# A long convolution with a small expert: two 1,024-blocks, folded transforms, mirrored tables and a list-scheduled order

## The chip, the cores and the metric

The kernel runs on one core of one Trainium2 chip. The metric is the device time of one execution in microseconds (us); lower is better. Each kernel that matters was run several times, in rounds in which the kernel before ran on the same chip.

Engines: PE is TensorE (PEld its weight loads), DVE is VectorE, ACT is ScalarE, SP issues the DMAs (SPq is its sequencer). "L374" is line 374 of the kernel. The first lines of helper functions stand for all their callers: L374 is every DVE product or sum of two tensors in the changed kernel, L385 every ACT operation.

## The reference, cut to what matters

```python
def _A_ref(u, A_re, A_im, B_re, B_im, C_re, C_im, log_dt, Dskip):   # u: 1 x 2048 x 512
    dt = jnp.exp(log_dt)[:, None]
    ...
    P = jnp.exp(logdA[:, :, None] * l[None, None, :])               # 512 channels x 128 states x 2048 lags
    K = jnp.einsum("dn,dnl,dn->dl", Cc, P, dB).real                 # a filter of 2048 lags for each channel
    ...                                                             # y = u convolved with K, by FFT
    y = y.transpose(0, 2, 1) + u * Dskip[None, None, :]
def _B_ref(x, w_r, w_gate, w_up, w_down):
    idx = jnp.argsort(-(x @ w_r), axis=-1)[:, :2]                   # the 2 rows that go to the expert
    ...                                                             # silu(x w_gate) * (x w_up), then w_down
g = _sigmoid((x * gate_w).sum(-1, keepdims=True))
return g * a + (1 - g) * b
```

Both kernels build K from two tables. A lag is written as t1 + t2 with 32 values of t1 and 21 of t2; exp(lag x) is then a product of a t1 entry and a t2 entry, and the sum over the 128 states is a matrix product over partitions. Each entry needs an exp (magnitude), a sine and a cosine (angle) and two products. Then u and K are transformed, multiplied and transformed back.

## The kernel before

Its helpers keep one record of the last write and of the readers for each buffer; an operation waits for all that the record says:

```python
class Sched:
    def _deps(self, eng, reads, writes):
        ...
        for b in reads:
            add(b.last_w)
        for b in writes:
            add(b.last_w)          # one record for the whole buffer
            for r in b.readers:
                add(r)
    ...
    def op(self, eng, fn, reads=(), writes=()):
        waits = self._deps(eng, reads, writes)
        ...                        # program order is the order of each engine
```

The tables, four lags at a time, with a ring of two angle groups; and the table matmuls, one channel for each weight load, four of them beside each other in 32-column strips:

```python
elif stage == 'exp':
    for i, t in enumerate(lags):
        ...
        ACTV(TP(0, 128, (slot0 + i) * 8, (512, HC // 8), (1, 8)), AL(0, 128, c0, (1, HC)), ACTF.Exp, [bAL], [bTP], scale=float(t))
...
def kgen_mm(hh):
    ...
    h.matmul(P32(b, 32 * c4, 32, cq * 24, (1, 24)), TP(0, 128, (ch // 8) * 512 + (ch % 8), (8, 32)),
             TQ(0, 128, ch, (HC, 24)), start=True, stop=False, tile_position=(0, 32 * c4))
```

All 32 exps of the first half write `bTP` (those of the second another buffer, `bEB`), so each waits for the one before, although they write different columns.

Of the kernel before, what the change touches and what calls it, by code (L numbers as in the profile page):

```python
# [27 lines left out]
class Buf:  # L28

    def __init__(self, name, parents=()):  # L30
        self.name = name
        self.last_w = None
        self.readers = []
        self.parents = list(parents)

    def prior(self):
        out = []
        for p in self.parents:
            if p.last_w is not None:
                out.append(p.last_w)  # L40
            out.extend(p.readers)
            out.extend(p.prior())
        return out


class Sched:
    def __init__(self, nc, block_sems):
        self.nc = nc
        self.ops = {e: [] for e in ENGS}
        self.sem = dict(block_sems)  # L50
        self.cnt = {e: 0 for e in ENGS}
        self.known = {e: {} for e in ENGS}
        self.dma_sems = []
        self.dma_free = []
        self.final_waits = []

    def _deps(self, eng, reads, writes):
        deps = {}
        def add(ev):
            if ev is None:  # L60
                return
            s, v = ev
            k = id(s)
            if self.known[eng].get(k, 0) >= v:
                return
            if k not in deps or deps[k][1] < v:
                deps[k] = (s, v)
        for b in reads:
            add(b.last_w)
        for b in writes:  # L70
            add(b.last_w)
            for r in b.readers:
                add(r)
            for r in b.prior():
                add(r)
        out = list(deps.values())
        for s, v in out:
            self.known[eng][id(s)] = v
        return out

    def _commit(self, ev, reads, writes):
        for b in reads:
            b.readers.append(ev)
        for b in writes:
            b.last_w = ev
            b.readers = []

    def op(self, eng, fn, reads=(), writes=()):
        waits = self._deps(eng, reads, writes)
        self.cnt[eng] += 1  # L90
        ev = (self.sem[eng], self.cnt[eng])
        self.ops[eng].append((fn, waits, (self.sem[eng], 1)))
        self._commit(ev, reads, writes)
        return ev

    def dma(self, fn, sem, n=1, reads=(), writes=(), eng=SP, final=False):
        waits = self._deps(eng, reads, writes)
        ev = (sem, 16 * n)
        self.ops[eng].append((fn, waits, (sem, 16)))
        self._commit(ev, reads, writes)  # L100
        if final:
            self.final_waits.append(ev)
        return ev

    def emit(self, eng, h):
        for fn, waits, inc in self.ops[eng]:
            for s, v in waits:
                h.wait_ge(s, v)
            r = fn(h)
            if isinstance(r, (list, tuple)):  # L110
                for i in r:
                    i.then_inc(inc[0], inc[1])
            else:
                r.then_inc(inc[0], inc[1])
        if eng == SP:
            for s, v in self.final_waits:
                h.wait_ge(s, v)


def sb(t, p0, npart, col, *dims):  # L120
    w = t.shape[1]
    ap = [[w, npart]] + [[s, c] for (s, c) in dims]
    return bass.AP(t, p0 * w + col, ap)


# [3 lines left out]


LQ_T1 = [8 * k for k in range(32)]
LQ_T2 = list(range(8)) + [256, 258, 260, 262, 264, 516, 520, 772, 776, 1032, 1288, 1544, 1800]
NSLOT = 24
BLK, NBLK = 512, 4
KUSE = [(0, 0), (0, 1), (0, 2), (0, 3), (1, 3), (1, 4), (2, 4), (3, 4), (3, 5)]
# [9 lines left out]
def theta():  # L145
    f = np.arange(BLK)
    return 2.0 * np.pi * (f + 0.5) / (2 * BLK)


def fwd_mats():  # L150
    th = theta(); t = np.arange(BLK)
    c = np.cos(np.outer(t, th)); s = -np.sin(np.outer(t, th))
    sg = np.where(np.arange(BLK) % 2 == 0, 1.0, -1.0)[None, :]
    return np.concatenate([c, s], 1), np.concatenate([-sg * s, sg * c], 1)


def inv_mat():
    th = theta(); t = np.arange(BLK)
    c = (2.0 / (2 * BLK)) * np.cos(np.outer(th, t)); s = -(2.0 / (2 * BLK)) * np.sin(np.outer(th, t))
    return np.concatenate([c, s], 0)  # L160


def kspec_mats(L=2048):
    lq = bf16_lag(np.arange(L))
    rep = {}
    for j, t2 in enumerate(LQ_T2):
        for k, t1 in enumerate(LQ_T1):
            q = t1 + t2
            if q not in rep:
                rep[q] = (j, k)  # L170
    th = theta()
    out = np.zeros((len(KUSE), 128, 2 * BLK))
    cover = np.zeros(L, dtype=bool)
    for u, (i, jg) in enumerate(KUSE):
        for g in range(4):
            j = 4 * jg + g
            if j >= len(LQ_T2):
                continue
            for k in range(32):
                q = LQ_T1[k] + LQ_T2[j]  # L180
                if rep.get(q) != (j, k):
                    continue
                ls = np.nonzero(lq == q)[0]
                ls = ls[(ls >= BLK * i) & (ls < BLK * (i + 1))]
                if len(ls) == 0:
                    continue
                cover[ls] = True
                t = ls - BLK * i
                out[u, 32 * g + k, :BLK] = np.cos(np.outer(t, th)).sum(0)
                out[u, 32 * g + k, BLK:] = -np.sin(np.outer(t, th)).sum(0)  # L190
    assert cover.all(), "some lags are not covered by KUSE"
    return out



L, D, NS = 2048, 512, 128
NTB, NCH, NF, HC = 16, 4, 1792, 256


class View:  # L200

    def __init__(self, arena, byte_off, nbytes, dt):
        a = arena[:, byte_off // 2:(byte_off + nbytes) // 2]
        self.base = a if dt == BF else a.bitcast(dt)
        self.row = self.base.ap[0][0]

    def __call__(self, p0, npart, col, *dims):
        return bass.AP(self.base.tensor, self.base.offset + p0 * self.row + col, [[self.row, npart]] + [[s, c] for (s, c) in dims])


def bass_gated_mix__ssm_conv_s4__moe_arch_mod__prompt_kernel(nc, A_u, A_A_re, A_A_im, A_B_re, A_B_im, A_C_re, A_C_im, A_log_dt, A_Dskip,
           B_x, B_w_r, B_w_gate, B_w_up, B_w_down, gate_w, out, dbg=None):
    dbg = dbg or {}
    ident_c = nc.inline_tensor(bf16_bits(np.eye(128, dtype=np.float32)), "c_ident").ap().bitcast(BF)
    cf = np.zeros((128, 160), np.float32)
# [19 lines left out]
    with ExitStack() as es:  # L235
# [115 lines left out]
        def kt(i):  # L351
            return KPT(0, 128, i * D, (1, D))
# [572 lines left out]
```

## Time and profile before

| | before |
|---|---|
| time | 375.66 us (375.5 to 375.82) |
| span of the profiled run | 373.4 us |
| DVE busy | 270.7 us, 72%, 495 instructions |
| ACT busy | 239.4 us, 64%, 385 |
| PE busy | 188.9 us, 51%, 3,674 |

The prediction below shows the engine shares, the slices and the durations. Two more lines of the kernel before, from its list of the costliest groups: after the names stand the count, then busy us and mean ns, then the idle time just ahead of the group and who ended it.

```profile
L670 PE MATMUL ps<-RT 128*32 128x24 bf16 x512 | 22.7, 286 | 52.1 <-DVE RT L306 52.1
...
L403 ACT ACTIVATE RT<-RS 128x256 int32<-128x256 f32 x64 | 26.4, 416 | 1.9
```

The first is half of the table matmuls: they wait 52 us for DVE's tables and are small. The second is part of the angle work: 64 scalings on ACT, beside 148 more on DVE.

### The profile page before, as it was taken

To read this page: it belongs to the slowest core of one execution; us is meant where nothing else is said; L and a number is where in the kernel's file an instruction comes from. 1 tells how busy PE (TensorE), PEld (TensorE's weight loads), DVE (VectorE), ACT (ScalarE), POOL (GpSimd) and SP (SyncE) were. 2 spreads that over 40 slices of the span, in tenths; PEclk is the share of its full clock that TensorE was granted. 3 is DMA by queue.
4 is the path that set the end of the run, shared out by engine and by line. 5 is a ranking of instruction groups with operands and counts; after the bars stand their busy time and mean duration, and the time that the engine had idled before them with its cause. 6 is when DMAs were issued, how large, how long until landed. Compare 5 with 4: busy or idle time off the path is not lost.

```text
span 373.4 us, 8503 instructions
## 1 busy us (share of the span) xinstructions
PE 188.9 (51%) x3674; PEld 170.3 (46%) x3674; DVE 270.7 (72%) x495; ACT 239.4 (64%) x385; POOL 1.7 (0%) x6
## 2 busy tenths in 40 slices
PE   2600301432300076704343803889899999998810
PEld 2500300330100076704343703789889889886810
DVE  0795658562599992878105999999999299899555
ACT  2899453399596999566999981553753484481461
POOL 0000010000000000000000000000000000000000
PEclk9855555555655556855856865689989969969785
DMA  6999000005000000000000000000000000200222
GB/s 154 275 443 438 26 3 0 0 11 187 0 1 0 0 4 5 2 1 2 1 2 0 2 0 2 4 4 4 2 2 2 3 2 2 58 3 2 58 67 45
DMA packets 18261, 16.91 MB, mean 45 GB/s; under 512 B 12848, under 2 KB 17072, under 8 KB 18096
## 3 DMA queue, kind: packets, MB, share of 16 engines
q1 hardware_dynamic: 18224, 16.37, 13.3%
q8 instruction: 29, 0.48, 0.5%
q14 instruction: 8, 0.07, 0.1%
HBM read 14.27 MB, written 2.10 MB: 44 GB/s over the span
## 4 chain that ended last, share of the span: by engine, by line
ACT 36%; DVE 32%; PE 26%; issue 4%; DMA 1%; SPq 1%; ACTq 0%; DVEq 0%
DVE RT L306 23%; ACT RT L316 21%; PE ps L739 10%; ACT RK L316 8%; PE ps L789 5%; DVE RT L310 5%; ACT L316 3%; PE ps L707 2%; ACT RT L837 2%; PE ps L670 2%; PE ps L674 1%; PE ps L779 1%; PE ps L778 1%; PE ps L607 1%; DVE RT L309 1%
## 5 line engine op out<-in xcount | busy, mean ns | idle before, releaser
L306 DVE TENSOR_TENSOR RT<-RT 128x1024 bf16<-128x1024 bf16 (+5 forms) x146 | 101.2, 704 | 29.7 <-ACT RT L316 19.3
L316 ACT ACTIVATE RT<-ps 128x512 bf16<-128x512 f32 (+3 forms) x79 | 51.8, 662 | 55.4 <-PE ps L739 22.8
L739 PE MATMUL ps<-RU,RC 128*128 128x128 bf16 x896 | 55.7, 228 | 16.7 <-ACT RK L316 16.6
L310 DVE TENSOR_SCALAR RT<-RS 128x256 int32<-128x256 f32 x148 | 49.2, 341 | 19.1 <-ACT RT L403 14.9
L739 PEld LDWEIGHTS ps<-RU,RC 128*128 128x128 bf16 x896 | 54.8, 103 | 17.1 <-issue 16.9
L306 DVE TENSOR_TENSOR RT<-RT,RK 128x4096 bf16<-128x4096 bf16 (+3 forms) x32 | 55.0, 1761 | 8.5 <-ACT RT L316 8.4
L316 ACT ACTIVATE RT<-RT 128x2048 bf16<-128x2048 int16 (+1 forms) x28 | 50.3, 1811 | 9.8 <-DVE RT L310 9.8
L670 PE MATMUL ps<-RT 128*32 128x24 bf16 x512 | 22.7, 286 | 52.1 <-DVE RT L306 52.1
L670 PEld LDWEIGHTS ps<-RT 128*32 128x32 bf16 x512 | 21.2, 171 | 52.9 <-DVE RT L306 52.4
L316 ACT ACTIVATE RT<-RS 128x256 bf16<-128x256 f32 x74 | 30.8, 416 | 3.5 <-DVE RS L306 1.2
L707 PE MATMUL ps<-RS,RC 128*128 128x128 bf16 x288 | 20.4, 240 | 20.2 <-ACT RS L316 17.6
L707 PEld LDWEIGHTS ps<-RS,RC 128*128 128x128 bf16 x288 | 19.5, 110 | 21.0 <-ACT RS L316 18.2
L316 ACT ACTIVATE RK<-ps 128x512 bf16<-128x512 f32 x32 | 19.1, 595 | 15.3 <-PE ps L707 5.9
L306 DVE TENSOR_TENSOR RT<-RT,RS 128x1024 bf16<-128x1024 bf16 (+1 forms) x48 | 27.8, 619 | 0.4
L789 PE MATMUL ps<-RT,RC 128*128 128x128 bf16 x384 | 27.7, 247 | 0.0
L403 ACT ACTIVATE RT<-RS 128x256 int32<-128x256 f32 x64 | 26.4, 416 | 1.9
L789 PEld LDWEIGHTS ps<-RT,RC 128*128 128x128 bf16 x384 | 27.2, 113 | 0.3
L837 ACT ACTIVATE RT<-RT,RS 128x128 bf16<-128x128 bf16 x48 | 19.2, 401 | 12.5 <-DVE RT L306 11.0
L674 PE MATMUL ps<-RT 128*32 128x24 bf16 x512 | 22.9, 286 | 3.8 <-issue 3.8
L674 PEld LDWEIGHTS ps<-RT 128*32 128x32 bf16 x512 | 21.8, 169 | 4.1 <-issue 4.1
L306 DVE TENSOR_TENSOR RT<-RK,RT 128x1024 bf16<-128x1024 bf16 x16 | 11.1, 691 | 13.2 <-ACT RT L316 12.9
L316 ACT ACTIVATE RK<-RS 128x256 bf16<-128x256 f32 x32 | 19.4, 605 | 1.0
(66 smaller groups left out, 189.8 us busy)
## 6 DMA issues: line engine op xcount, KB each, us to landing
RC<-c_mats SPq DMA_DIRECT2D x1, 5376.0 KB, 24.5
RU<-in_A_u_dram SPq DMA_DIRECT2D x4, 512.0 KB, 8.0
RK<-in_B_w_gate_dram SPq DMA_DIRECT2D x1, 1792.0 KB, 9.4
RK<-in_B_w_up_dram SPq DMA_DIRECT2D x1, 1792.0 KB, 13.4
RK<-in_B_w_down_dram SPq DMA_DIRECT2D x1, 1792.0 KB, 7.5
out_dram<-RT SPq DMA_DIRECT2D x3, 512.0 KB, 3.8
out_dram<-RT SPq DMA_DIRECT2D x4, 128.0 KB, 2.0
RT<-in_A_A_re_dram SPq DMA_DIRECT2D x1, 128.0 KB, 2.6
```

Of the source, the lines that this page charges most:

```text
L306: return S.op(eng, lambda h: h.tensor_tensor(out=o, in0=a_, in1=b_, op=op), reads=rd, writes=wr)
L309: return S.op(eng, lambda h: h.tensor_scalar(out=o, in0=a_, scalar1=s1, scalar2=None, op0=op0), reads=rd, writes=wr)
L310: return S.op(eng, lambda h: h.tensor_scalar(out=o, in0=a_, scalar1=s1, scalar2=s2, op0=op0, op1=op1), reads=rd, writes=wr)
L316: return S.op(ACT, lambda h: h.activation(out=o, in_=a_, func=func, scale=scale), reads=rd, writes=wr)
L403: S.op(ACT, lambda h, i=i, t=t, cs=cs: h.activation(out=ARG(0, 128, ((gi * 2 + cs) * 4 + i) * HC, (1, HC)), in_=B16(0, 128, c0, (1, HC)), ...
L607: last = h.matmul(P32(by_, 0, 2, 0, (1, D)), HB(0, 128, 6 * 28 + fb * 2, (1, 2)), WD(0, 128, fb * D, (1, D)), start=(fb == 0), stop=(fb == ...
L670: h.matmul(P32(b, 32 * c4, 32, cq * 24, (1, 24)), TP(0, 128, (ch // 8) * 512 + (ch % 8), (8, 32)), TQ(0, 128, ch, (HC, 24)), start=True, s ...
L674: last = h.matmul(P32(b, 32 * c4, 32, cq * 24, (1, 24)), TP(0, 128, (ch // 8) * 512 + 256 + (ch % 8), (8, 32)), TQ(0, 128, NSLOT * HC + ch ...
L707: last = h.matmul(P32(bb[hb_], 0, 128, tl * 128, (1, 128)), CM(0, 128, OF_KP + u * 1024 + tau * 128, (1, 128)), KC(0, 128, kb * 768 + KUSE ...
L739: last = h.matmul(P32(bb[hb_], 0, 128, tl * 128, (1, 128)), CM(0, 128, of + tc * 1024 + tau * 128, (1, 128)), U(0, 128, tb * D + ck * 128, ...
L789: last = h.matmul(P32(b, 0, 128, tt * 128, (1, 128)), CM(0, 128, OF_G + sc * 512 + tt * 128, (1, 128)), YHs[vb](0, 128, j * 1024 + sc * 12 ...
L837: S.op(ACT, lambda h, tb=tb, vb=vb: h.activation(out=YA(0, 128, vb * 2048 + tb * 128, (1, 128)), in_=YA(0, 128, vb * 2048 + tb * 128, (1, ...
```

## The change

The intent is less work on DVE and ACT, and an order in which the engines wait less.

- Blocks of 1,024 in place of 512, with even and odd samples transformed apart and then folded: four block products become two, and the mixing steps go.
- t1 runs over 16 values and their mirror images 31 - k, so 16 angles serve 32 entries. The cosine comes from the sine of a folded angle (a magnitude step, `max(-x, x)` on 16-bit halves). The 13 far t2 entries are complex products of the 8 near ones with entries at 8 multiples of 256, so they need 8 angles and not 13.
- The table matmuls take 4 channels for each weight load: 128 columns of weights, of which 4 diagonal blocks of the result are used.
- Dependences are recorded for pieces of a buffer, by key. All operations are collected first; a list scheduler then fixes the order of each engine at build time from assumed durations.

The core of the diff (cut; hunks that only move or rename are left out):

```diff
-LQ_T1 = [8 * k for k in range(32)]
-LQ_T2 = list(range(8)) + [256, 258, 260, 262, 264, 516, 520, 772, 776, 1032, 1288, 1544, 1800]
+T1 = [8 * k for k in range(16)] + [8 * (31 - k) for k in range(16)]
+ANG1 = [124 - 8 * s for s in range(16)]
+T2 = list(range(8)) + [256, 258, 260, 262, 512, 516, 768, 772, 1024, 1280, 1536, 1792, 2048]
...
-                        ACTV(TP(0, 128, (slot0 + i) * 8, (512, HC // 8), (1, 8)), AL(0, 128, c0, (1, HC)), ACTF.Exp, [bAL], [bTP], scale=float(t))
+                AC(TP[h](0, 128, 32 * HC + s * HC, (1, HC)), AL(0, 128, h * HC, (1, HC)), ACTF.Exp, [AL], [(TP[h], ("e", s))], scale=float(T1[s]), tset=ts)
...
-                                h.matmul(P32(b, 32 * c4, 32, cq * 24, (1, 24)), TP(0, 128, (ch // 8) * 512 + (ch % 8), (8, 32)), TQ(0, 128, ch, (HC, 24)),
-                                         start=True, stop=False, tile_position=(0, 32 * c4))
+                            last = hh.matmul(pb(0, 128, (g - b0) * 84, (1, 84)), TP[h](0, 128, part * 32 * HC + g, (64, 128)),
+                                             TQ[h](0, 128, part * NJ * HC + g, (64, 4), (HC, NJ)), start=(part == 0), stop=(part == 1))
...
+        P.span = P.schedule()
+        P.emit(sems, dsem)
```

`HC` is 256, the channels of a half; `NJ` is 21. The text of the changed kernel creates its operations in this order, which the scheduler then rearranges: exps and first list of half 0, routing, forward transforms, second list of half 0, exps and first list of half 1, table matmuls of half 0, second list of half 1, first kernel spectra, table matmuls of half 1, first products, second kernel spectra, first inverse, then products and inverse of half 1.

## The prediction

> **What bounds the kernel now.** I read the page first (engine shares, slices, chain), then the groups by line with shapes kept apart, then the chain in order of time and a few stretches of the timeline.
>
> ```profile
> PE 188.9 (51%) x3674; PEld 170.3 (46%) x3674; DVE 270.7 (72%) x495; ACT 239.4 (64%) x385; POOL 1.7 (0%) x6
> ...
> DVE  0795658562599992878105999999999299899555
> ACT  2899453399596999566999981553753484481461
> ...
> PEclk9855555555655556855856865689989969969785
> ...
> ACT 36%; DVE 32%; PE 26%; issue 4%; DMA 1%; SPq 1%; ACTq 0%; DVEq 0%
> ```
>
> No engine is full. The chain is split between ACT, DVE and PE: in the first 60% ACT and DVE hand each other small pieces (tables of exp, sin, products), then DVE products and PE transforms alternate. The tensor clock is at half in most of that part. So the kernel is bound by a relay of two engines, and what counts is DVE work plus the places where DVE waits for ACT or PE.
>
> The durations that I price the new kernel with, from the groups by shape:
>
> ```profile
> L310 DVE TENSOR_SCALAR RT<-RS 128x256 int32<-128x256 f32 x148 | 49.2, 341 | 19.1 <-ACT RT L403 14.9
> L306 DVE TENSOR_TENSOR RT<-RT 128x1024 bf16<-128x1024 bf16 x72 | 48.8, 689 | 17.9 <-ACT RT L316 16.5
> L306 DVE TENSOR_TENSOR RT<-RT 128x2048 bf16<-128x2048 bf16 x14 | 17.1, 1224 | 7.6 <-ACT RT L837 7.0
> L306 DVE TENSOR_TENSOR RT<-RT 128x512 bf16<-128x512 bf16 x24 | 10.2, 424 | 3.4 <-ACT RT L316 2.9
> L312 DVE SCALAR_TENSOR_TENSOR RT<-RT 128x512 f32<-128x512 f32 x2 | 1.4, 692 | 0.1
> L316 ACT ACTIVATE RT<-RT 128x2048 bf16<-128x2048 int16 x26 | 49.3, 1904 | 9.8 <-DVE RT L310 9.8
> L316 ACT ACTIVATE RT<-ps 128x512 bf16<-128x512 f32 x64 | 37.8, 596 | 44.9 <-PE ps L739 22.8 <-PE ps L789 12.9 <-DVE RT L306 6.5
> L837 ACT ACTIVATE RT<-RT,RS 128x128 bf16<-128x128 bf16 x48 | 19.2, 401 | 12.5 <-DVE RT L306 11.0
> ```
>
> Read: shape, count, busy us and mean ns. And from the timeline, what a row of small ones costs start to start, and what happens beside the 32-column table matmuls:
>
> ```profile
> 12.53 14.31 ACT L316 ACTIVATE RT<-RS 128x256 bf16<-128x256 f32 x32 [1.22 <-DVE RS L306]
> ...
> 230.30 13.24 DVE L306 TENSOR_TENSOR RT<-RT,RK 128x4096 bf16<-128x4096 bf16 x2
> ...
> 265.77 4.49 DVE L306 TENSOR_TENSOR RT<-RT,RK 128x4096 bf16<-128x4096 bf16 x2
> ```
>
> 32 exps take 14.31 us, 447 ns each, though one is recorded as 416. The same two DVE products take 13.24 us at 230 us and 4.49 us at 266: in the first stretch the table matmuls (1,024 of them in this half, 32-column weights, strided reads) run on PE, so something in those reads slows DVE almost threefold. ACT's exps show it too (605 ns instead of 416 beside the first half).
>
> **The Trainium skill.** "VectorE: DVE Perf Modes", section "The perf-mode tier table", gives bf16 tensor_tensor 2x (1224 ns at 2048) and fp32 1x; the trace agrees (1224; fp32 of 512 at 687). "ScalarE: Activation LUTs", section "What ACT_TABLE_LOAD costs", gives 186 ns + 0.833 ns per element, 93 more per pointer operand, and 1283 for a table load: agreed (1904 at 2048 against 1892; 401 at 128 with a pointer scale against 386; loads 1283); but it says that back-to-back ACTIVATEs overlap by 93 ns, and here the pitch is 31 ns longer than the record, so I use 447. "TensorE: Matmul & The Clock Gate", section "Back-to-back issue gap", gives N/2.4+2.5 ns warm: the trace has 224 matmuls of 128 columns in 12.5 us, 56 ns. "DMA: Bandwidth & Descriptors", section "Latency and other measured facts", has 261 GB/s for a DMA transpose, contiguous 350 to 400; no transpose is in this trace.
>
> **The change, part by part.** Counts are from the built instruction streams.
>
> DVE work:
> - Set-up: 5 fp32 products of 512 (0.69), two scalings (0.43), three of 1024 with an fp32 side (estimate 1.22): 8.
> - Tables: per half 16 angle groups' work. First list, 4 groups: abs as scalar_tensor_tensor on 1024 (1x: [...]scaled from 692 at 512, 1.22), negation 0.45, two products of 2048 (1.22): 4.1 a group, plus four angle scalings of 0.3 in half 0 (half 1 has them on ACT). Second list: 4 x (1.22 + 2 x 0.69) + 12 x 0.69 for weights + far lags 12 x 0.69 + 12 x 0.42 + 6 x 0.29 = 33.8. Two halves: 2 x (16.5 + 33.8) + 32 x 0.3 = 110. Before: 148 scalings (49) and some 170 products for the same.
> - Folding the spectra: 32 of 512: 13.6. Products: per half and quarter 8 of 2048 and 8 of 1024, 15.3, four times 61. Inverse with gate: 32 from PSUM on 256, estimate 0.43: 13.7. Routing, small ops: 8.
> - Sum 214, against 270.7. Diagonals, mixing and the four-block accumulations are gone.
>
> ACT work: 96 exps and 32 scalings at 0.447: 57; 32 sines of 1024 at 1.04 (1.13 with a pointer bias): 35; PSUM copies, 32 of 1024 at 1.02, 22 of about 500, 16 of 512 with pointer (0.69), others: 63; 8 table loads 10; small 1. Sum 166 against 239.
>
> PE: about 1,280 matmuls for 3,674. Columns streamed stay about 220 thousand (144 x 512 forward, 224 x 256 kernel spectra, 256 x 256 inverse, 32 x 512 update, 256 x 84 table), 92 us warm, twice that cold. The 2,048 matmuls with 32 columns become 256 with 128 columns and 84 moving.
>
> The list-scheduled order is fixed at build, so I walked the three streams by hand from wait to wait. Stages of the path:
> 1. Start. The queue now loads the forward matrix (2.1 MB) and U (2.1 MB) first: about 13 us at 380 GB/s. Then comes U a second time by DMA transpose (2.1 MB) and only after it the parameters (0.8 MB), transposed too. In the profile 256-byte rows moved at some 130 to 230 GB/s; I take 150 for the transposes: first parameter at about 29 us, last at 34. DVE's set-up in stream order is 9.5 us from the first to the magnitude: exps can start at 40 us. (Before: at 12.5.) PE runs the forward transform meanwhile, which is off the path.
> 2. 32 exps (14.3) with 4 PSUM copies (4.1), a load (1.3), first sine and cosine (2.2): to 62.
> 3. First list of half 0 on DVE, with the angles for the next: 8 x 1.22, 16 x 0.3, 4 x 1.22, 4 x 0.45, four folds, gaps: 24, and 2 of waiting for the second exps: to 88.
> 4. Second list of half 0: 36.5 plus 26 ns a step: 38, to 126.
> 5. Half 1's exps write where the expert's weights lie, so they wait for the expert's last matmul, which stands behind six of eleven groups of table matmuls: 72 x 0.13 = 9.4, and 4. Then 32 exps with 5 copies (17.3), load and first sines (3.5): 34 us with DVE mostly idle: to 160.
> 6. First list of half 1: 17, to 177. Then ACT's second exps with 4 copies and two loads: DVE waits about 13: to 190. Second list 35: to 225.
> 7. Products of half 0: 31 and 2 of waiting for half 1's spectra (table matmuls 16, selection 6, first spectrum 8 run beside it): to 258.
> 8. Products of half 1 with 16 of the gate steps: 30.6 + 6.9 + 1 = 38: to 296.
> 9. Tail: the last block's 64 inverse matmuls of 256 columns (7), two gate steps (0.9), output (2): to 306.
> Contention by the table matmuls: they read about half as many elements as before (128 x 212 against 1,024 x 56 a half), where the excess was 8.7 us; 3 us of it on DVE in stage 7. Profile span 309, and the timed run was 2 us longer than the span before: 311. DVE steps with no wait between them overlap a little (two of 2048 in 2.35 us instead of 2.45), worth about 3. I say 308 us, 18% less than 375.66.
>
> **The rivals.**
> (a) DVE becomes the bound throughout: the scheduler fills it, and the time is 214 plus a start of 35 and a tail of 10, about 260 to 270. For: before, DVE ran at 90% from 200 to 270 us. Against: the stream order in stages 5 and 6 has every DVE step behind an exp or sine; I count about 45 us of idle there.
> (b) The DMA transposes set the start: at 40 GB/s the parameters come at about 85 us and all shifts by 50: about 355. For: they are one queue, and no run has shown one. Against: the skill's 261. At 40 GB/s the gain would shrink to 5%.
> (c) The strided table matmuls still starve DVE and ACT, threefold over 15 us twice: +10 to +15, about 320. For: the trace's 13.24 against 4.49. Against: a quarter as many weight loads, no column tiles.
> (d) PE cold everywhere: forward and kernel spectra are hidden, the inverse tail and the table matmuls would add 10 to 15.
>
> **Range and chances.** The DVE and ACT durations are all measured; the doubt is in the start (-6 to +20), contention (-3 to +10), stage 5 (+-5) and the clock (0 to +10): more up than down. (a) could take 25 off. So 286 to 334. Slower than before by 2% (383) needs the transposes at about 30 GB/s: 2%; within 2%: 2%; faster: 96%.
>
> **What would show it.** Right: DVE busy 205 to 225, ACT 155 to 175; first exp at 34 to 45 us; a DVE gap of 15 to 25 us near 130 to 160 released by ACT, and one of about 10 near 180; last product 10 us before the end. Wrong: transposes landing after 40 us; DVE steps of 1024 well above 689 ns beside the table matmuls; DVE idle under 40 us in all (rival a); a PSUM gate step far from 0.43; forward matmuls holding up the folds.

## The result, and the profile after

| | before | after |
|---|---|---|
| time, median | 375.74 us (375.5 to 377.54, 4 runs) | 293.25 us (292.37 to 294.04, 4 runs) |
| span of the profiled run | 373.4 us | 291.4 us |
| DVE busy | 270.7 us | 194.2 us |
| ACT busy | 239.4 us | 143.4 us |
| PE busy | 188.9 us | 191.5 us |
| DVE idle (span less busy) | 102.7 us | 97.2 us |

The ratio is 0.7802, with a 95% interval of 0.7772 to 0.7832: 22% less time. A ratio here is the mean time of one kernel's runs over the mean of the other's in the same rounds, so it is not quite the ratio of the medians in the table. Executions over 1.5% slower than the fastest of the same kernel are left out of the means.

The head of the page of the changed kernel: busy us of each engine with its share and count, then the busy tenths and the granted TensorE clock in 40 slices of the span, then the chain that ended last.

```profile
PE 191.5 (66%) x1298; PEld 126.6 (43%) x1298; DVE 194.2 (67%) x347; ACT 143.4 (49%) x252; POOL 0.2 (0%) x4
...
DVE  0001796699799998110059619999991099999993
...
PEclk9999956959758655575555555589855579997999
...
DVE 38%; PE 32%; ACT 16%; SPq 9%; issue 3%; DMA 1%; DVEq 0%
```

In the DVE row there are long runs of 9 and three holes: the first three slices, "1100" at 117 to 146 us, and "10" at 219 to 233 us. The relay of small pieces between ACT and DVE takes less of the chain: ACT's part of the chain fell from 36% to 16%, and PE's rose from 26% to 32%.

The groups with shapes kept apart (count, busy us, mean ns, idle ahead and its releaser), to set beside those in the prediction:

```profile
L374 DVE TENSOR_TENSOR AR<-AR 128x1024 bf16<-128x1024 bf16 x96 | 60.9, 697 | 11.7 <-ACT AR L385 11.2
...
L381 DVE SCALAR_TENSOR_TENSOR AR<-AR 128x1024 int16<-128x1024 int16 x16 | 22.1, 1379 | 0.1
L381 DVE SCALAR_TENSOR_TENSOR AR<-ps,AR 128x256 bf16<-128x256 f32 x32 | 13.1, 475 | 2.4 <-PE ps L785 2.4
...
L385 ACT ACTIVATE AR<-AR 128x256 bf16<-128x256 f32 x96 | 30.8, 415 | 15.3 <-DVE AR L374 11.5 <-PE ps L652 3.7
...
L694 PE MATMUL ps<-AR 128*128 128x84 bf16 x256 | 47.9, 371 | 14.9 <-DVE AR L374 14.9
L694 PEld LDWEIGHTS ps<-AR 128*128 128x128 bf16 x256 | 45.0, 180 | 17.6 <-DVE AR L374 15.0 <-issue 0.4 <-ACT AR L385 0.4
```

Look at count and busy together. 96 products of 1024 are recorded with 697 ns each, which would be 66.9 us end to end; the engine was busy 60.9. Consecutive steps overlap. The 96 exps are recorded with 415 ns, which would be 39.8 us; ACT was busy 30.8. And the 256 table matmuls took 47.9 us of PE, about as much as before's 1,024 (22.7 for the half shown above, 22.9 for the other).

The timeline of the changed kernel (start, duration, engine, line, operation, shape, count, and in brackets the idle time just before). First ACT and SP, then DVE, then PE:

```profile
43.85 5.00 ACT L385 ACTIVATE AR<-AR 128x256 bf16<-128x256 f32 x16
```

```profile
4.75 16.66 SPq L448 DMA_TRANSPOSE AR<-in_A_u_dram  x4
```

```profile
148.57 0.43 DVE L378 TENSOR_SCALAR AR<-AR 128x1024 bf16<-128x1024 bf16 x1 [19.41 <-ACT AR L385]
...
173.49 0.69 DVE L374 TENSOR_TENSOR AR<-AR 128x1024 bf16<-128x1024 bf16 x1 [8.80 <-ACT AR L385]
...
178.25 11.70 DVE L374 TENSOR_TENSOR AR<-AR 128x1024 bf16<-128x1024 bf16 x19
...
233.17 7.41 DVE L374 TENSOR_TENSOR AR<-AR 128x2048 bf16<-128x2048 bf16 x8 [13.23 <-ACT AR L385]
```

```profile
205.80 23.73 PE L694 MATMUL ps<-AR 128*128 128x84 bf16 x128
```

Sixteen exps take 5.00 us, 313 ns each, where the same exps took 447 ns before. Four transposing DMAs of u hold the queue for 16.66 us, and the parameters come after them. On DVE, 19 products of 1024 take 11.70 us, 616 ns each. The brackets carry the waits: 19.41 us at 148.57 (the last of several in which the expert, the first half's table matmuls and the second half's exps follow each other), 8.80 at 173.49 (the second list's exps), and 13.23 at 233.17. The last one reads "<-ACT", but ACT only copies what PE finishes: PE ran the second half's table matmuls from 205.80 to 229.53 us, and a piece of the first half's kernel spectrum, whose copy DVE needed, stood behind them.

### The profile page after: what moved, and what is told of

The parts are those of the page before. It is cut to its first block, busy times and chain, and to the rows that moved or that the text cites. A ratio compares the mean times of both kernels' runs of the same rounds, so it can differ in the third digit from the quotient of the medians.

```text
span 291.4 us, 3307 instructions
## 1 busy us (share of the span) xinstructions
PE 191.5 (66%) x1298; PEld 126.6 (43%) x1298; DVE 194.2 (67%) x347; ACT 143.4 (49%) x252; POOL 0.2 (0%) x4
## 4 chain that ended last, share of the span: by engine, by line
DVE 38%; PE 32%; ACT 16%; SPq 9%; issue 3%; DMA 1%; DVEq 0%
DVE AR L374 29%; PE ps L694 15%; ACT AR L385 14%; PE ps L735 6%; DVE AR L381 6%; SPq L448 6%; DVE AR L378 3%; PE ps L785 2%; PE ps L652 2%; PE ps L669 2%; PE ps L803 2%; PE ps L802 2%; ACT L231 2%; SPq L388 1%; DMA AR<-in_A_B_re_dram 1%
## 5 line engine op out<-in xcount | busy, mean ns | idle before, releaser
L374 DVE TENSOR_TENSOR AR<-AR 128x1024 bf16<-128x1024 bf16 (+6 forms) x222 | 146.6, 728 | 59.5 <-ACT AR L385 56.0
L385 ACT ACTIVATE AR<-AR 128x256 bf16<-128x256 f32 (+5 forms) x164 | 75.1, 542 | 31.7 <-DVE AR L374 11.5
L385 ACT ACTIVATE AR<-ps 128x1024 bf16<-128x1024 f32 (+6 forms) x64 | 50.7, 806 | 78.3 <-PE ps L694 31.0
L669 PE MATMUL ps<-AR 128*128 128x512 bf16 x128 | 37.9, 443 | 31.2 <-ACT AR L385 17.1
L694 PE MATMUL ps<-AR 128*128 128x84 bf16 x256 | 47.9, 371 | 14.9 <-DVE AR L374 14.9
L694 PEld LDWEIGHTS ps<-AR 128*128 128x128 bf16 x256 | 45.0, 180 | 17.6 <-DVE AR L374 15.0
L669 PEld LDWEIGHTS ps<-AR 128*128 128x128 bf16 x128 | 13.8, 112 | 50.5 <-ACT AR L385 18.4
L735 PE MATMUL ps<-AR 128*128 128x256 bf16 x224 | 34.0, 289 | 0.7 <-ACT AR L385 0.7
L785 PE MATMUL ps<-AR 128*128 128x256 bf16 x256 | 30.2, 281 | 4.4 <-DVE AR L381 4.4
L785 PEld LDWEIGHTS ps<-AR 128*128 128x128 bf16 x256 | 25.5, 101 | 8.8 <-DVE AR L381 5.0
L735 PEld LDWEIGHTS ps<-AR 128*128 128x128 bf16 x224 | 22.0, 101 | 12.9 <-issue 2.9
L378 DVE TENSOR_SCALAR AR<-AR 128x256 int32<-128x256 f32 (+5 forms) x48 | 12.7, 327 | 21.8 <-ACT AR L385 21.6
L381 DVE SCALAR_TENSOR_TENSOR AR<-AR 128x1024 int16<-128x1024 int16 (+2 forms) x20 | 22.8, 1148 | 0.1
L802 PE MATMUL ps<-AR 128*128 128x512 bf16 x16 | 9.3, 578 | 17.1 <-ACT AR L385 17.1
L381 DVE SCALAR_TENSOR_TENSOR AR<-ps,AR 128x256 bf16<-128x256 f32 x32 | 13.1, 475 | 2.4 <-PE ps L785 2.4
L802 PEld LDWEIGHTS ps<-AR 128*128 128x128 bf16 x16 | 1.7, 105 | 22.5 <-ACT AR L385 20.5
L707 PEld LDWEIGHTS ps<-AR 128*32 128x32 bf16 x96 | 3.9, 122 | 16.3 <-ACT AR L385 14.6
L672 PE MATMUL ps<-AR 128*128 128x512 bf16 x16 | 7.1, 443 | 0.0
```

What stands on the lines that cost most here:

```text
L374: return P.op(DVE, lambda h: h.tensor_tensor(out=o, in0=a, in1=b, op=op), rd, wr, cost=tt_cost(o, a, b), **k)
L378: return P.op(DVE, lambda h: h.tensor_scalar(out=o, in0=a, scalar1=s1, scalar2=None, op0=op0), rd, wr, cost=c, **k)
L381: return P.op(DVE, lambda h: h.scalar_tensor_tensor(out=o, in0=a, scalar=sc, in1=b, op0=op0, op1=op1), rd, wr, cost=0.16 + nel(o) * 1.04e- ...
L385: return P.op(ACT, lambda h: h.activation(out=o, in_=a, func=func, scale=scale, bias=bias), rd, wr, cost=0.185 + nel(o) * 0.833e-3 + (0.09 ...
L669: last = h.matmul(pb(0, 128, par * 512, (1, 512)), F(0, 128, ((par * 4 + st) * 2 + part) * 512 + ft * 128, (1, 128)), U(0, 128, (blk * 8 + ...
L694: last = hh.matmul(pb(0, 128, (g - b0) * 84, (1, 84)), TP[h](0, 128, part * 32 * HC + g, (64, 128)), TQ[h](0, 128, part * NJ * HC + g, (64 ...
```

## The experiments

Twelve kernels ran. All gave results within the reference's tolerance except x_kgwm. Two other kernels with wrong tables, x_kgw and b_kgw, passed the comparison all the same: the convolution is a small part of the output. So for x_perm and x_best, which change the table layout and mean to be right, the comparison says little.

Theories about what made the gain, as they stood before the runs: (1) the waits and the order, that is, steps that no longer wait for an unrelated predecessor and a schedule that gives DVE something to do; (2) the arithmetic that was taken out. And about what holds the changed kernel at 293 us: the expert's place in the order, the table matmuls' pace, the late parameters, or the dependences themselves.

### x_waw: each exp waits for the one before again

```diff
+                    if o.tag == "chain" and kn.get(ACT, 0) < o.pos:
+                        waits.append((ACT, o.pos))
+                        kn[ACT] = o.pos
                     vc = dict(kn)
```

The 96 exps carry the tag; order and all else are the same.

> The changed kernel in the same order, with each of the 96 exps made to wait for the ACT instruction in front of it, as every exp of the kernel before does. Theory 1 (the wait on the own predecessor makes the difference of 447 ns and 313 ns between starts): runs of exps go from 313 to about 447 ns a piece, ACT busy hardly changes, and of 96 x 0.134 = 12.9 us some 8 to 12 us lie on the path: 301 to 305 us. Theory 2 (it is the other destination layout, or one tensor for all): 313 ns stays, 293 us within 1.

Measured: 304.2 us (302.86 to 304.68), ratio to before 0.8083 [0.8046, 0.8119], against 0.7802 for the changed kernel. ACT's timeline in this run:

```profile
45.49 7.15 ACT L388 ACTIVATE AR<-AR 128x256 bf16<-128x256 f32 x16
```

The same 16 exps take 7.15 us in place of 5.00: 447 ns each, the pace of the kernel before, with nothing changed but the wait. It costs 11 us.

### x_dvewait: each DVE step waits for the one before

```diff
+                    if e == DVE and kn.get(DVE, 0) < o.pos:
+                        waits.append((DVE, o.pos))
+                        kn[DVE] = o.pos
                     vc = dict(kn)
```

> The changed kernel with one more wait: every DVE step waits for the DVE step before it, so that no two overlap; orders, counts and shapes are the same. It tests the term by which the prediction missed most, the pace of the second lists (0.715 us a product of 1024, where the changed kernel shows 0.61). Theory 1: the prediction's prices were right for steps that wait, and the overlap that the finer records of reads and writes allow is what it missed: 20 products of 1024 take 14 us again, the stretches where DVE sets the end grow by 12 to 22 us, and the time is 305 to 316. Theory 2: the pace comes from elsewhere (operand layout, fewer readers): under 298.

Measured: 317.34 us (316.46 to 318.52), ratio 0.8421 [0.8376, 0.8466]. DVE's timeline:

```profile
192.44 13.98 DVE L377 TENSOR_TENSOR AR<-AR 128x1024 bf16<-128x1024 bf16 x19
```

19 products: 13.98 us where the changed kernel has 11.70, so 736 ns a step and not 616, at a recorded duration of 695 and 697. The step that waits costs 0.12 us more. Theory 1 stands, and the cost is a little above its range: 24 us. The Trainium skill, "Perfetto Trace Analysis", section "Optimizing Scalar/DVE Operations", says why: the recorded duration holds a write-acknowledgement half that overlaps with the next instruction, about 60 ns for DVE on SBUF. The trace agrees in kind, with 81 ns of overlap (697 less 616) and another 41 ns lost when a wait stands between (736 less 695).

### b_nowait: the kernel before without its same-engine waits in the tables

```diff
-            add(b.last_w)
+            add(b.last_w, True)      # True: not waited for when it is this engine's own, in the 'arg' and 'exp' stages
```

> The kernel before with one thing changed: table exps and angle scalings, which write disjoint slots, no longer wait for the instruction of their own engine in front of them. Theory 1 (the wait costs 134 ns each on ACT): 32 exps in about 10.0 us instead of 14.3, 170 such ACT steps save 23 us of ACT, of which some 8 to 15 on the path: 361 to 368 us. Theory 2 (the distance of 447 ns is that of the kernel's layout): 375 us within 1.

Measured: 361.08 us (360.24 to 361.94), ratio 0.9608 [0.9573, 0.9643]. Its first exps:

```profile
12.32 9.92 ACT L319 ACTIVATE RT<-RS 128x256 bf16<-128x256 f32 x32 [1.22 <-DVE RS L309]
```

32 exps in 9.92 us in place of 14.31. So 14.6 us of the 82 could be had in the old kernel by finer records alone.

### x_prog: the changed kernel in the order of its text

```diff
         P.span = P.schedule()
+        for e in ENGS:
+            P.order[e].sort(key=lambda o: o.idx)
```

> The changed kernel with the list-scheduled order taken out: every engine keeps its own operations, but in the order in which the program text creates them (results stay right). Theory 1: the order carries a large part of the gain, as the text makes one angle group at a time and DVE then waits for each sine: 330 to 370 us, DVE busy unchanged at 194, its idle time up by 40 to 75 us. Theory 2: the arithmetic removed from DVE and ACT (77 and 96 us of busy time) is the gain, and the order only polishes: under 310 us.

Measured: 363.79 us (361.95 to 366.28 in three fast runs; a fourth, 367.62, counts as slow), ratio 0.9661 [0.9574, 0.9748]. DVE's longest waits in the timeline of this run:

```profile
207.31 1.34 DVE L381 SCALAR_TENSOR_TENSOR AR<-AR 128x1024 int16<-128x1024 int16 x1 [31.90 <-ACT AR L385]
...
305.42 0.88 DVE L381 SCALAR_TENSOR_TENSOR AR<-ps,AR 128x256 bf16<-128x256 f32 x2 [33.68 <-PE ps L785]
```

DVE is busy 200.4 us, much as in the changed kernel (194.2), but idle 161.6 us of its span of 362.0. In the text order the second half's second list waits 31.90 us, since ACT makes its exps only after it has copied out all of the first half's table matmuls, and the gate steps of the first half stand in front of the second half's products and wait 33.68 us for the inverse transform. Theory 1 stands: with 70 us less DVE work than before (200.4 against 270.7) and 92 us less ACT work (147.7 against 239.4), the text order gains 3.4%. This does not make the scheduler worth 71 us against any hand order: the text was written for a scheduler. It shows that the removed work alone does not shorten the time; the order turns it into time.

### x_kspec: the delayed piece of the first kernel spectrum moved ahead

```diff
         P.span = P.schedule()
+        move(PE, [557], 559)     # last spectrum piece of half 0 ahead of half 1's table matmuls
+        move(ACT, [558], 560)    # and its copy
```

> The changed kernel with one group of 8 kernel-spectrum matmuls of half 0, and its PSUM copy, moved in front of the table matmuls of half 1 on PE and ACT. Theory 1 (that group alone makes DVE wait 13.2 us near 220 us): the wait goes and the time falls by 11 to 13, to about 281. Theory 2 (the chain of 128 table matmuls, selection and first spectra of half 1 on PE ends at about 240 us anyway, and DVE would only wait there instead): a new wait of 6 to 9 us in front of half 1's products, and a fall of 3 to 6, to 287 to 290.

Measured: 295.55 us (294.54 to 296.21), ratio 0.7862 [0.7831, 0.7893]: no gain. Both theories missed. DVE and PE in the timeline:

```profile
245.60 20.41 DVE L374 TENSOR_TENSOR AR<-AR 128x2048 bf16<-128x2048 bf16 x21 [15.86 <-ACT AR L385]
```

```profile
208.27 23.73 PE L694 MATMUL ps<-AR 128*128 128x84 bf16 x128
```

The move did what it should: DVE's rest of the first half's products no longer waits. But those 12 products were also the work that DVE had while PE made the second half's spectra. In the changed kernel DVE waits 13.23 us and then has work up to the end; here it works first and then waits 15.86 us. The table matmuls on PE (23.73 us, starting 2.5 us later than the 205.80 of the changed kernel) and what follows them set the end in both. A wait that is taken away ahead of the same PE work comes back behind it.

### x_ffn: the expert moved early

```diff
+        move(DVE, [148, 150, 207, 208, 211, 212, 203, 204], 285)   # the expert's and the forward transform's small steps
+        move(PE, [154], 419)                                        # its last matmuls ahead of the table matmuls
+        move(ACT, [218] + list(range(315, 347)), 420)               # half 1's 32 exps ahead of the copies
...
```

(Some more moves place ACT's copies of the table matmuls between its sines.)

> The changed kernel with the expert's last steps (two small DVE copies, a Silu, the product and the last matmul) and six spectrum folds moved ahead of the end of the second list of half 0, the 32 exps of half 1 put right behind the last sine of half 0, and the table PSUM copies spread among the sines that follow. Theory 1 (exps of half 1 wait only for the expert's last matmul, which sits behind the table matmuls): DVE's wait of about 20 us before half 1's first list falls to under 5, and the time by 25 to 31, to 262 to 268. Theory 2 (ACT is short of time there whatever the order, PSUM copies and sines): half of the gap stays, fall of 10 to 15, 278 to 283.

Measured: 276.72 us (275.05 to 277.61), ratio 0.7358 [0.7321, 0.7395], a fall of 16.5 us, between the two theories. DVE's two waits that are left, and what the first of them stands behind on ACT:

```profile
146.99 1.33 ACT L385 ACTIVATE AR<-AR 128x256 bf16<-128x256 f32 x4 [1.23 <-PE ps L713]
```

```profile
154.65 0.69 DVE L374 TENSOR_TENSOR AR<-AR 128x1024 bf16<-128x1024 bf16 x1 [14.81 <-ACT AR L385]
...
215.00 30.27 DVE L374 TENSOR_TENSOR AR<-AR 128x2048 bf16<-128x2048 bf16 x33 [14.02 <-ACT AR L385]
```

The wait of 19.41 us is gone (2.31 us are left there), so the order of that stretch was its cause. The expert, the exps of half 1 and the copies were moved together, so the share of the expert's place alone is not separated. The wait for the second list grew from 8.80 to 14.81: the exps at 146.99 write where the first half's table result lies, and PE's selection from it (L713) released them. That is memory used twice, not an order that could be chosen freely. The wait of 14 us behind the second set of table matmuls is untouched.

### x_kgw and x_kgwm: the table matmuls read contiguous operands (wrong)

```diff
-    TP[h](0, 128, part * 32 * HC + g, (64, 128))
+    TP[h](0, 128, part * 32 * HC + g * 128, (1, 128))          # both runs: weights
-    TQ[h](0, 128, part * NJ * HC + g, (64, 4), (HC, NJ))
+    TQ[h](0, 128, part * NJ * HC + g * 84, (1, 84))            # x_kgwm only: the moving operand too
```

> Wrong results on purpose: the table matmuls of the changed kernel load 128 neighbouring columns as weights instead of columns 64 elements apart; counts, shapes and waits are the same. Theory 1: the strided weight load sets their pace (0.182 us each, 23.7 us for the second half's 128): they fall to 16 us or less, and since DVE waits behind the second half's and ACT behind the first half's, the span falls 8 to 14 us from 291.4. Theory 2: the moving operand's stride or the half clock sets the pace: 22 to 24 us as before, and the span stays within 1%.

> Wrong results on purpose: as the run with neighbouring weight columns, and the moving operand of 84 columns contiguous too. That run went from 0.185 to 0.145 us for each table matmul. Theory 1: strided reads, of weights and of the moving operand, are all that keeps the tensor engine's pace down: 0.10 us or less, 13 us for the second half's 128, and a span of 272 to 278. Theory 2: the rest is the half clock[...]: no change from 18.6 us, and a span of 279 to 284.

Measured, one look each: 283.34 us with contiguous weights (span 281.5), 262.30 with both contiguous (span 260.5). The table matmuls' groups in the two runs, x_kgw first:

```profile
L694 PE MATMUL ps<-AR 128*128 128x84 bf16 x256 | 37.5, 321 | 15.1 <-DVE AR L374 15.1
```

```profile
L694 PE MATMUL ps<-AR 128*128 128x84 bf16 x256 | 13.7, 220 | 16.7 <-DVE AR L374 15.0 <-ACT AR L385 1.6
```

The same 256 matmuls take 47.9 us as they are, 37.5 with contiguous weights, 13.7 with both contiguous; 24 of them in 1.07 us, or 45 ns each, in the last run at full clock. The span falls by 9.9 and 30.9 us. Theory 1 of x_kgw held for the span, but not for the pace (18.57 us for the second half's 128, where it said 16). Theory 1 of x_kgwm was right in kind and too small in size; theory 2, that the half clock sets the pace, fell, and the traces settle it, since the granted clock changes within each run. In x_kgw 72 of these matmuls took 10.49 us at a clock of 0.50 (108.3 to 118.7 us), 146 ns each, and 24 took 3.62 us at 1.00 (124.0 to 127.6 us), 151 ns each: twice the clock, and no faster. With both operands contiguous the clock does count: in x_kgwm 72 took 5.04 us at 0.53 (108.8 to 113.7 us), 70 ns each, against the 45 ns at 1.00 (116.8 to 117.9 us).

The Trainium skill, "SBUF — State Buffer", section "Door 1: The DMA port swizzle", speaks of 16-byte lines in SBUF: at least two accesses to a line are needed for full bandwidth. The weights here are 128 bytes apart and the moving elements 512, one access to a line. The traces agree in kind, with a factor of 3.5 in all, of which a part is the clock's, as just seen.

### b_kgw: the kernel before with contiguous table weights (wrong)

```diff
-    TP(0, 128, (ch // 8) * 512 + (ch % 8), (8, 32))
+    TP(0, 128, ch * 32, (1, 32))
```

> Wrong results on purpose: the kernel before, with its 32-column table weights loaded from neighbouring columns instead of columns 8 elements apart; the moving operand as before. Theory 1: the strided weight reads are what slows DVE beside them: its two products of 4096 that took 13.24 us at 230 us fall to 4.5 to 6, and the span falls 5 to 15 us from 373.4. Theory 2: the slowing comes from something else in that stretch (the moving reads, or the shape of these products): they stay at 12 us or more, and the span within 1%.

Measured, one look: 376.29 us, span 374.5. DVE in this run, beside the same table matmuls that slowed it before:

```profile
230.33 7.75 DVE L306 TENSOR_TENSOR RT<-RT,RK 128x4096 bf16<-128x4096 bf16 x2
...
298.27 2.29 DVE L306 TENSOR_TENSOR RT<-RT,RK 128x4096 bf16<-128x4096 bf16 x1 [11.23 <-ACT RT L316]
```

The two products fall from 13.24 to 7.75 us, where they take 4.49 undisturbed. The four after them, which now run beside table matmuls too, take 3.79 and 3.80 us a pair in place of 2.49 and 3.43. All six together save 3.8 us of the excess of 8.75, so the strided weight reads made some 44% of it. But the span did not fall. DVE reached its next wait at 287.0 us, 3.5 us earlier, and then waited 11.23 us, where the kernel before waited 6.73 at the same place. So neither theory was right as a whole: the mechanism holds and the gain is zero, since another wait takes it back.

### x_resched: the scheduler given measured durations, parameters first, the expert with priority

```diff
-            return 0.157 + nel(o) * (0.52e-3 if fast else 1.04e-3)
+            return 0.09 + nel(o) * (0.52e-3 if fast else 1.04e-3)
-                        cost=0.185 + nel(o) * 0.833e-3 + (0.09 if not isinstance(scale, float) else 0), **k)
+                        cost=0.1 + nel(o) * 0.833e-3 + (0.09 if not isinstance(scale, float) else 0), **k)
-    [], [(PRM, i)], cost=0.07, nbytes=131072)
+    [], [(PRM, i)], cost=1.25, nbytes=131072, prio=1000.0)
-                P.op(PE, mm, [TP[h], TQ[h]], [pb.buf], cost=ng * 2 * 0.1)
+                P.op(PE, mm, [TP[h], TQ[h]], [pb.buf], cost=ng * 2 * 0.16)
...
```

> The changed kernel with the same operations, and the durations that the list scheduler assumes set to what the trace shows: DVE and ACT steps without the wait between independent ones (0.09 and 0.10 us beside the elements instead of 0.157 and 0.185), table matmuls 0.16 instead of 0.10, 1.25 and 2.4 us of queue time for each transposing DMA instead of 0.07; the parameters are loaded first and the expert's matmuls get priority. Theory 1: the rest of the idle time on DVE (97 us of 291) is mostly what wrong durations and the late parameters made of the order: exps start before 20 us, and the time is 252 to 266 us. Theory 2: the idle time is in the dependences themselves (expert before half 1's exps, table matmuls before the last products): 268 us or more, no better than moving the expert by hand (276.7).

Measured: 276.80 us (275.39 to 278.11), ratio 0.7343 [0.7301, 0.7386]. From its timeline, ACT's first exps and DVE's two longest waits:

```profile
16.56 9.91 ACT L385 ACTIVATE AR<-AR 128x256 bf16<-128x256 f32 x32 [10.39 <-DVE AR L374]
```

```profile
115.01 0.77 DVE L374 TENSOR_TENSOR AR<-AR 128x512 bf16<-128x512 bf16 x2 [12.03 <-ACT AR L385]
...
210.38 2.48 DVE L374 TENSOR_TENSOR AR<-AR 128x2048 bf16<-128x2048 bf16 x2 [15.26 <-ACT AR L385]
```

The exps start at 16.56 us, 23 us earlier than in the changed kernel, and the time is that of x_ffn. This is the time of theory 2. The trace suggests that the early start is given back around the table matmuls, 12 us beside the first set and 15 behind the second (PE ran them at 99.66 to 123.32 and 183.14 to 206.80 us). Three things were changed at once here, so their shares are not separated.

### x_perm: x_ffn with a table layout that feeds the matmuls

The weights stay as they are. The short-lag table is written in another channel order, so that the four channels of one matmul are neighbours in it.

```diff
-    AC(TQ[h](0, 128, NJ * HC + i * HC, (1, HC)), AL(0, 128, h * HC, (1, HC)), ACTF.Exp, ...
+    AC(TQ[h](0, 128, NJ * HC + i * HC, (4, 64), (1, 4)), AL(0, 128, h * HC, (1, 64), (64, 4)), ACTF.Exp, ...
-    TQ[h](0, 128, part * NJ * HC + g, (64, 4), (HC, NJ))
+    TQ[h](0, 128, part * NJ * HC + 4 * g, (HC, NJ), (1, 4))
...
```

> Right results meant: the version with the expert moved early (276.7 us), and the short-lag table kept in another channel order, so that the 4 channels of one table matmul are neighbours in it: its moving operand is read in runs of 4 elements (8 bytes) instead of single elements 512 bytes apart; the weights keep their stride of 64 elements. It tells apart which of the two strided reads costs the most, after both contiguous gave 0.046 us a matmul, and weights alone 0.145. Theory 1: the moving operand's jumps of 512 bytes are the main cost: 0.12 us or less for each, the 128 of the second half in 15 us, and 256 to 268 us. Theory 2: weights and moving operand cost alike, each hides behind the other, so the strided weights alone hold it at 0.14 to 0.18: 269 to 278 us.

Measured: 271.64 us (271.34 to 272.29), ratio 0.7206 [0.7152, 0.7259]. The second set of table matmuls, DVE's waits for the second list and behind those matmuls, and the exps with strided reads:

```profile
197.51 11.58 PE L701 MATMUL ps<-AR 128*128 128x84 bf16 x128
```

```profile
163.08 0.69 DVE L374 TENSOR_TENSOR AR<-AR 128x1024 bf16<-128x1024 bf16 x1 [18.39 <-ACT AR L385]
...
211.85 30.27 DVE L374 TENSOR_TENSOR AR<-AR 128x2048 bf16<-128x2048 bf16 x33 [1.35 <-ACT AR L385]
```

```profile
73.32 8.73 ACT L385 ACTIVATE AR<-AR 128x256 bf16<-128x256 f32 x16
```

The 128 matmuls fall from 23.7 to 11.58 us, 90 ns each, although the weights keep their stride: the moving operand's jumps of 512 bytes were the larger cost when the other was strided too. DVE's wait behind them falls from 14.02 to 1.35 us. But the exps that fetch their input in the new order take 8.73 us for 16 where sequential ones take 5.01, and DVE waits 18.39 us for them where x_ffn had 14.81, and 6.15 where it had 2.10. So 12.7 us gained and 7.6 given back leave 5.1: theory 1's pace, theory 2's time.

### x_best: the two together

x_resched's kind of schedule (table matmuls now assumed at 0.12 us) with x_perm's layout; ACT reads in sequence and writes with the stride.

```diff
-    AC(TQ[h](0, 128, NJ * HC + i * HC, (4, 64), (1, 4)), AL(0, 128, h * HC, (1, 64), (64, 4)), ACTF.Exp, ...
+    AC(TQ[h](0, 128, NJ * HC + i * HC, (1, 4), (4, 64)), AL(0, 128, h * HC, (64, 4), (1, 64)), ACTF.Exp, ...
...
```

> What the runs point to, together: the order scheduled anew (parameters first, the expert with priority, durations near the measured ones) with the short-lag table in the channel order that lets the table matmuls read runs of 4; the exps and scalings now write with the stride and read in sequence, since the version with strided reads had them at 487 ns a piece where sequential ones take 415. Theory 1: with table matmuls at 0.09 us the idle of DVE behind both sets (12 and 15 us in the rescheduled version) falls by half or more, and the two gains add: 250 to 264 us. Theory 2: strided writes slow ACT as strided reads did, and the order of memory reuse keeps DVE waiting for the second half's long-lag exps: 265 to 275.

Measured: 261.42 us (261.10 to 262.61), ratio 0.6951 [0.6900, 0.7001]. It is the fastest of all: 0.6951 over 0.7802 is 0.89 of the changed kernel. The page's first line, and from the timeline ACT's strided exps and DVE's two longest waits:

```profile
PE 168.2 (65%) x1298; PEld 106.0 (41%) x1298; DVE 196.1 (75%) x348; ACT 154.0 (59%) x252; POOL 0.2 (0%) x4
```

```profile
47.32 8.28 ACT L385 ACTIVATE AR<-AR 128x256 bf16<-128x256 f32 x14
```

```profile
114.52 0.76 DVE L374 TENSOR_TENSOR AR<-AR 128x512 bf16<-128x512 bf16 x2 [11.20 <-ACT AR L385]
...
149.38 0.69 DVE L374 TENSOR_TENSOR AR<-AR 128x1024 bf16<-128x1024 bf16 x1 [12.08 <-ACT AR L385]
```

The wait behind the second set of table matmuls fell from x_resched's 15.26 to 2.50 us. The time is 10 us under x_perm's, so the early start seems to count now; that is argued, since the two differ in the whole schedule. Theory 1 held for the time and only half for the waits: the one at 114.52, beside the first set, is hardly shorter than the 12.03 of x_resched. Strided writes are no cheaper for ACT than strided reads (591 ns each against 546 and, in sequence, 313). DVE is still idle 63.8 us of the span. What is left open: whether a copy of the parameters in the new order, made once, would take back the ACT time; the kernel's memory plan has no room for it as it stands.

## Why the prediction was right, and where its steps were off

The time, 293.25 us, lies in the range of 286 to 334; the point of 308 was 15 us too high. By the prediction's own stages (its last one given there as 306 before the additions):

| stage ends | predicted | measured | difference that this stage adds |
|---|---|---|---|
| 1 first exp | 40 | 39.6 | -0.4 |
| 2 first fold of half 0 | 62 | 57.0 | -4.6 |
| 3 first list, half 0 | 88 | 79.7 | -3.3 |
| 4 second list, half 0 | 126 | 108.9 | -8.8 |
| 5 expert, exps of half 1 | 160 | 148.6 | +5.7 |
| 6 both lists, half 1 | 225 | about 201 | -12.5 |
| 7 and 8 products | 296 | 279.5 | +7.5 |
| 9 tail | 306 | 291.4 | +2 |

- **The start (stage 1) was right.** The queue was busy with u's transposes and then the parameters; first exp predicted at 40 us, measured at 39.58. Rival (b), transposes at 40 GB/s, fell. x_resched suggests that this start was not worth what it seems: 23 us earlier, and the time of x_ffn.
- **The mis-sized term: the pace of independent steps.** Stages 2, 3, 4 and 6 priced exps at 447 ns and products of 1024 at 715 (689 and 26 for the step). They run at 313 and 616. The kernel before could not show that pace for the exps, since it waited in each; the prediction took a pitch with a wait in it for the engine's own. The skill's sentence that back-to-back activations overlap by 93 ns was on its table and was overruled by the trace of before. It holds about where no wait stands between: 415 recorded, 306 from start to start (16 starts in the 4.90 us from 43.85 to the copy at 48.75), an overlap of 109 ns. x_waw and x_dvewait put the waits back and add 11 and 24 us, more than the whole miss. The prediction allowed "about 3" for DVE's overlap.
- **Stage 5 had the mechanism and was 5.7 us short.** The exps of half 1 behind the expert behind the table matmuls: x_ffn moved the expert and those exps, and the wait went. The short term is mostly the table matmuls, 72 in 13.43 us (0.187 each; the 0.13 of the prediction is not derived there): 4.0 of the 5.7 us.
- **Stages 7 and 8 missed a wait.** Two us of waiting for half 1's spectra were predicted, 13.23 came. The table matmuls were given 16 us "beside" the products and took 23.7, and the order put a piece that DVE needed behind them. x_kspec shows that the order of that piece was not the cause; x_kgwm and x_perm show that the matmuls' pace was (in x_perm the wait is 1.35 us).
- **Counts in its working.** The kernel before has 512 table matmuls a half, 1,024 in all (the page counts 512 at each of L670 and L674); the prediction says 1,024 and 2,048. So its ground for 3 us of contention in place of 8.7, half as many elements read, does not hold: it is 128 x 212 = 27,136 against 512 x 56 = 28,672. Its columns streamed add up to 234 thousand and not 220, off its path. Its second list is 33.8 in the sum of the work and 36.5 in stage 4, which it does not explain.
- **Sums.** DVE busy: 205 to 225 predicted, 194.2; ACT: 155 to 175 predicted, 143.4. Overlap is much of it, since time in which two steps overlap counts once: with the waits put back DVE is busy 220.6 us (x_dvewait) and ACT 153.7 (x_waw). The gate step was 475 ns where 430 was estimated, the magnitude step 1,379 where 1,220 was.
- **Rival (a), DVE full throughout, did not come:** DVE was idle 97 us, where the prediction counted some 45 in stages 5 and 6 and a start of 35. x_best, at 261, is where (a) put the time (260 to 270), and even there 64 us of DVE are idle.
- **Rival (c), DVE starved by strided matmuls, did not come** either: products of 2048 in the changed kernel have a mean of 1,241 ns, against 1,224 before (1,288 for the nine in the window of 205.8 to 220 us, beside the second set). Since the elements read are nearly as many as before, why they slow DVE so little here stays open. The strided reads hurt PE itself. The prediction looked at the right trace line, 13.24 against 4.49, and drew only half of what it says; b_kgw shows that the strided weights were part of the cause there.
- **Rival (d), a cold PE adding 10 to 15 us,** has about the right size for the wrong reason. The table matmuls were slow at a clock of 0.50 and no faster where it was higher (24 of them in 4.62 us at 0.83, 192 ns each): the reads set their pace.

The two large misses have opposite signs, some 30 us too slow in the table stages and some 13 us too fast around the table matmuls. That is luck in the sum, and the table shows it where the total does not.

Two things are shown and one is only argued. Shown: with all the work removed and the text's order the time is 364 us, and with the list schedule 293. Shown: the pace of single steps depends on the waits between them. Argued only: how the 82 us divide between arithmetic and order, since the two were not separated the other way round (the old arithmetic under the list scheduler was not built).

## What to carry to other kernels

Before you price a new kernel from an old one's trace, see whether the old step waits for its predecessor; its pitch is then not the engine's. Work that is taken out shortens a kernel only where the order lets the next thing come forward: the moved wait of x_kspec and the faster products of b_kgw gained nothing, and x_resched, with its early start, came out no faster than x_ffn. And count the bytes between neighbouring elements of a matmul's operands: here the layout of a table was worth 12 us on one set of 128 matmuls, and its price has to be paid where the table is written.

## What the Trainium skill lacked or had wrong

- "ScalarE: Activation LUTs": the overlap of about 93 ns between activations is right only without a wait on the one before. Measured: 313 ns each without, 447 with, at a record of about 415 in both.
- "Perfetto Trace Analysis", on scalar and DVE operations: it has the overlap of DVE steps (81 ns measured for products of 1024, about 60 stated), but not that a wait on the engine's own last step costs more than the overlap: 736 ns a step against a record of 695. "VectorE: DVE Perf Modes", too, has no cost for such a wait.
- "SBUF — State Buffer" has the 16-byte lines without a price for a matmul's operands, and "TensorE: Matmul & The Clock Gate" gives none either. Measured for 128 columns of weights and 84 of data: 185 ns with strides of 128 and 512 bytes, 145 with contiguous weights, 90 with strided weights and a moving operand in runs of 8 bytes, and with both contiguous 45 at full clock and 70 at a clock of 0.53.
- No page says that the granted clock can fall under a row of matmuls that the record shows as unbroken. In the changed kernel's second set, at 185 ns each, it was 0.79 from 205.9 to 212 us and 0.50 from 212 to 229.3; in that of x_perm, at 90 ns each, it was 1.00 (197.5 to 209 us). Nor does a page say that a starved matmul is no slower at half the clock: 146 ns at 0.50 and 151 at 1.00 in x_kgw.
- No page has ACT's price for a strided operand: an exp of 256 elements went from 313 ns to 546 with reads 256 bytes apart, and to 591 with writes 8 bytes apart.
- "DMA: Bandwidth & Descriptors" gives a bandwidth for DMA transposes and decode times for some, but not how long large ones from DRAM hold the issuing queue: 16.66 us of SP for four of 512 KB in the changed kernel.
